# Empty turns ahead of the first matmuls in each batch's transforms, the three uses of one PSUM bank moved within a block, and a down projection four steps behind

## The chip, the cores and the metric

The kernel runs on one core of one Trainium2 chip. The metric is device time in microseconds (us), the median of several executions.

## What is computed

The reference gates a long convolution and puts an MLP behind it, cut to what matters:

```python
h_filt = (np.maximum(pos_emb @ w1, 0.0) @ w2) * np.exp(-0.01 * pos)[:, None]   # 12480 x 128
u = x * v                                                # x, v: 4 batches x 12480 x 128
y = irfft(rfft(u, n=2*S) * rfft(h_filt, n=2*S))[:, :S]   # along the 12480 positions
t = (x * y).reshape(49920, 128)
h = t @ w_in                                             # 128 -> 2048
g = np.where(h > 0, h, np.exp(np.minimum(h, 0)) - 1)     # ELU
return g @ w_out                                         # 2048 -> 128
```

## The kernel before

The convolution is done with discrete Fourier transforms written as matmuls, in two stages with a round trip through DRAM between them. In fp32 a matmul is done as three (`mm3`, lines 53 to 55): operands are split into a rounded part (names ending in `_h`) and a remainder (`_l`), and high by high, low by high and high by low are summed.

For one batch, `stage1` takes 15 groups of 4 positions: `load` brings `xt` and `vt` (SP's queue), `gate` multiplies them on GpSimd (line 102, in place in `vt`), `split` rounds to `u_h` on ScalarE and takes the remainder `u_l` on VectorE, and four `mm3` per group write `aps`, which ScalarE and VectorE copy to `a_sb`; `store` writes it to DRAM, `a_d`. `stage2` takes 52 groups: it loads a table `t`, the stored `al` and the filter's spectrum `f`, rounds the table to `th` and `tl`, multiplies (`xps`), forms products `p` with the spectrum on VectorE and sums them on GpSimd (lines 420 and 421), transforms back (`bps`) and stores to `b_d`. Both are generators: each `yield` ends a piece, and whoever drives them gets one piece at a time.

Batch 0 goes through both stages alone, together with the filter and the splitting of the weights. Then the class `Mlp` runs 960 steps: 120 blocks (30 for each batch) of 4 x 104 tokens, 8 steps a block, each step for 256 of the 2048 hidden features. Step (j, c) issues, in this order:

- `up_proj`: six matmuls of 416 columns to `fps` (two buffers while transforms run, a third after), then two ScalarE instructions for `n` (lines 551 and 552);
- `split_lo` of two steps earlier: VectorE's remainder `g_l` (line 567);
- `elu`: VectorE's `g` (line 558) and GpSimd's cast to `g_h` (line 561);
- `down_proj` of `LAG` steps earlier: six matmuls that add to `ops`; behind the last of a block ScalarE copies `ops` to `o_sb`;
- pieces of the next batch's transforms (`side`), as many as keep their count at `SHARE` times the steps of this batch so far, until they run out. Blocks of batch 0 run beside the transforms of batch 1, and so on; those of batch 3 run alone;
- at fixed steps c of a block the work that prepares and ends blocks: `conv_out` of the next block (the last inverse transform, `yps`, six matmuls, and the gate `att`), `load` for the block three on, `split_b`, `transp` (four transposes to `tps`, then `t_h` and `t_l`), `finish` of the previous block (four transposes to `otp`, copied to `ost`), and `store`, the output transfer.

`yps`, `tps` and `otp` share one PSUM bank, the pool `psm` with one buffer. Every engine works through its instructions in program order, and so does SP's queue of transfers; the order in which this code is written is thus the order on each engine.

Of the kernel before, what the change touches and what calls it, by code (L numbers as in the profile page):

```python
# [27 lines left out]
DFF = 2048  # L28
NF = DFF // 128
NP = NF // 2  # L30
LAG = 3
NBK = 2 * NG
SHARE = 1.04
FWD = ((0, 1), (2, 0))
INV = ((3, 4), (5, 3))

# [2 lines left out]
def fftconv_gate_elu_mlp_kernel(ctx: ExitStack, tc: tile.TileContext, x, v, pos_emb, w1, w2,  # L39
# [41 lines left out]
    def stage1(st, h, ps_pool, ps_tag, first):  # L81
# [6 lines left out]
        def load(g):  # L88
            if g >= NG:
                return  # L90
            xt = xv.tile([N1, 2, G, D], F32, tag="xt", name="xt")
            vt = xv.tile([N1, 2, G, D], F32, tag="vt", name="vt")
            nc.sync.dma_start(out=xt, in_=xq[:, :, h, g * G:(g + 1) * G, :])
            nc.sync.dma_start(out=vt, in_=vq[:, :, h, g * G:(g + 1) * G, :])
            ld[g] = (xt, vt)

        def gate(g):
            if g >= NG:
                return
            xt, vt = ld[g]  # L100
            e = nc.vector if first and g < 2 else nc.gpsimd
            e.tensor_tensor(out=vt, in0=xt, in1=vt, op=ALU.mult)

        def split(g):
            if g >= NG:
                return
            vt = ld.pop(g)[1]
            u_h = up.tile([N1, 2, G, D], F32R, tag="u_h", name="u_h")
            u_l = up.tile([N1, 2, G, D], F32R, tag="u_l", name="u_l")
            copy(u_h, vt)  # L110
            nc.vector.tensor_tensor(out=u_l, in0=vt, in1=u_h, op=ALU.subtract)
            us[g] = (u_h, u_l)
# [7 lines left out]
        if first:  # L120
            filt = Filter(st)
            for g in range(4):
                filt.load(g)
                if g < 3:
                    load(g)
                filt.load_w(g)
            gate(0)
            gate(1)
            for q in range(3):
                filt.step(0, q)  # L130
        else:
            load(0)
            load(1)
            gate(0)
            gate(1)
        split(0)
        for g in range(NG):
            if first:
                gate(g + 2)
            u_h, u_l = us.pop(g)  # L140
            for i in range(4):
                r, w = divmod(i, 2)
                f = FWD[w][r]
                if w == 0:
                    a_sb = ap.tile([N1, G, Z, 2, D], F32 if first else F32R, tag="a_sb", name="a_sb")
                if first:
                    q = 2 * g + r
                    filt.step(q + 1, 2 * w)
                ps = ps_pool.tile([N1, 512], F32, tag=ps_tag, name="aps")
                mm3(ps, dft_h[:, f, :], dft_l[:, f, :], u_h[:, w], u_l[:, w])  # L150
                src = ps.rearrange("p (n d) -> p n d", n=G)
                if first and w == 0:
                    nc.vector.tensor_copy(out=a_sb[:, :, 0, w], in_=src)
                else:
                    copy(a_sb[:, :, 0, w], src)
                if not first:
                    nc.vector.tensor_tensor(out=a_sb[:, :, 1, w], in0=src, in1=a_sb[:, :, 0, w], op=ALU.subtract)
                if first:
                    if w == 0:
                        filt.step(q + 1, 1)  # L160
                        filt.load(q + 4)
                        filt.load_w(q + 4)
                    else:
                        filt.transform(q)
                        filt.weights(q)
                        filt.split_w(q - 1)
                if w == 0:
                    store()
                else:
                    stores.append((g, r, a_sb))  # L170
                if i == 0:
                    load(g + (3 if first else 2))
                if i == 1:
                    split(g + 1)
                if i == 2 and not first:
                    gate(g + 2)
                yield
# [143 lines left out]
    def stage2(st, h, ps_pool, ps_tag, first):  # L321
# [125 lines left out]
            load_t(g)  # L447
        for g in range(d):
            load_a(g)
        split_t(0)  # L450
        split_a(0)
        for g in range(NK):
# [19 lines left out]
    class Mlp:  # L472
        def __init__(self, st):
            self.xp = st.enter_context(tc.tile_pool(name="xp", bufs=3))
            self.bl = st.enter_context(tc.tile_pool(name="bl", bufs=2))
            self.b0 = st.enter_context(tc.tile_pool(name="b0", bufs=2))
            self.tq = st.enter_context(tc.tile_pool(name="tq", bufs=2))
            self.ep = st.enter_context(tc.tile_pool(name="ep", bufs=2))
            self.gp = st.enter_context(tc.tile_pool(name="gp", bufs=4))
            self.op = st.enter_context(tc.tile_pool(name="op", bufs=2))  # L480
            self.psf = st.enter_context(tc.tile_pool(name="psf", bufs=2, space=PS))
            self.pso = st.enter_context(tc.tile_pool(name="pso", bufs=1, space=PS))
            self.psm = st.enter_context(tc.tile_pool(name="psm", bufs=1, space=PS))

        def run(self, side, alone):
# [108 lines left out]
            def store():  # L594
                if outs:
                    j, o = outs.pop(0)
                    b, w, n = blocks[j]
                    nc.sync.dma_start(out=oq[:, w, b, n * G:(n + 1) * G, :], in_=o)
# [10 lines left out]
            done = 0  # L609
            for s in range(len(steps) + LAG):  # L610
                now = steps[s] if s < len(steps) else None
                if s == (NB - 1) * per:
                    psf2 = alone()
                if now:
                    up_proj(*now)
                if 2 <= s <= len(steps) + 1:
                    split_lo(*steps[s - 2])
                if now:
                    elu(*now)
                if s >= LAG:  # L620
                    down_proj(*steps[s - LAG])
                p, q = divmod(s, per)
                if q == 0:
                    done = 0
                while p in side and done < (q + 1) * SHARE:
                    done += 1
                    if next(side[p], None) is END:
                        del side[p]
                if now:
                    j, c = now  # L630
                    if c == 1:
                        conv_out(j + 1)
                        load(j + 3)
                    if c == 2:
                        split_b(j + 2)
                    if c == 4:
                        transp(j + 1)
                    if c == 5:
                        finish(j - 1)
                    if c == 7:  # L640
                        store()
            finish(ALL - 1)
            store()

# [92 lines left out]
```

## Time and profile before

| what | value |
|---|---|
| median of three runs | 3637.33 us (3637.32 to 3637.77) |
| the profiled execution: its time, its span | 3646.31 us, 3644.5 us |
| mean granted TensorE clock | 0.967 |
| TensorE matmul busy | 3434.0 us, 94% |
| TensorE weight load busy | 3158.4 us, 87% |
| VectorE busy | 3136.5 us, 86% |
| ScalarE busy | 2418.3 us, 66% |
| GpSimd busy | 2276.2 us, 62% |
| transfers | 646.29 MB, 177 GB/s as a mean |

In the profile's rows PE is TensorE's matmul, PEld its weight load, DVE VectorE, ACT ScalarE, POOL GpSimd and SPq the queue of transfers that SyncE issues. A row of the timeline has its start, its duration, the engine and line, the instruction with output<-inputs, and in brackets how long the engine stood idle before it and what ended that. Matmuls overlap in a pipeline, so a row's duration is longer than the distance to the next. In the trace the first step of the MLP runs at 553.4 us; the pieces of batch 1's transforms run beside it from there, the first matmuls of those of batches 2 and 3 start at 1402.9 and 2213.5 us. The last store of each batch's second stage is issued at 1312.0, 2124.2 and 2934.1 us; from there to the next start the MLP is alone.

### The profile page before, as it was taken

To read this page: it belongs to the slowest core of one execution; us is meant where nothing else is said; L and a number is where in the kernel's file an instruction comes from. 1 tells how busy PE (TensorE), PEld (TensorE's weight loads), DVE (VectorE), ACT (ScalarE), POOL (GpSimd) and SP (SyncE) were. 2 spreads that over 40 slices of the span, in tenths; PEclk is the share of its full clock that TensorE was granted. 3 is DMA by queue.
4 is the path that set the end of the run, shared out by engine and by line. 5 is a ranking of instruction groups with operands and counts; after the bars stand their busy time and mean duration, and the time that the engine had idled before them with its cause. 6 is when DMAs were issued, how large, how long until landed. Compare 5 with 4: busy or idle time off the path is not lost.

```text
span 3644.5 us, 53113 instructions
## 1 busy us (share of the span) xinstructions
PE 3434.0 (94%) x18444; PEld 3158.4 (87%) x18444; DVE 3136.5 (86%) x3941; ACT 2418.3 (66%) x3290; POOL 2276.2 (62%) x1578
## 2 busy tenths in 40 slices
PE   7887878989999999989999999989999999999999
PEld 5666767879998998879999998879999999999998
DVE  5647988989999988989999988979999988888887
ACT  3334546866666677866666677866666677777776
POOL 3406875857777765557766756657666655655555
PEclk8769998999999999999999999999999999999999
DMA  6648886767777735778888846778888832222220
GB/s 186 185 127 241 267 242 194 222 181 201 203 205 208 201 109 165 242 202 220 238 221 229 227 114 185 241 199 225 233 228 232 237 88 60 59 66 60 69 59 24
DMA packets 383995, 646.29 MB, mean 177 GB/s; under 512 B 24679, under 2 KB 170439, under 8 KB 374367
## 3 DMA queue, kind: packets, MB, share of 16 engines
q1 hardware_dynamic: 383305, 642.73, 62.4%
q8 instruction: 146, 2.39, 0.3%
q14 instruction: 123, 1.00, 0.1%
q10 hardware_dynamic: 421, 0.16, 0.0%
HBM read 412.76 MB, written 230.03 MB: 176 GB/s over the span
## 4 chain that ended last, share of the span: by engine, by line
PE 76%; DVE 8%; ACT 4%; DMA 4%; issue 4%; POOL 3%; SPq 0%; POOLq 0%; DVEq 0%; ACTq 0%
PE fps L53 9%; PE fps L55 9%; PE fps L54 9%; PE ops L53 9%; PE ops L54 9%; PE ops L55 8%; PE bps L439 4%; DVE g_l L567 2%; PE xps L53 2%; PE xps L54 2%; PE xps L55 2%; PE yps L53 2%; PE yps L54 2%; PE yps L55 2%; PE otp L589 1%
## 5 line engine op out<-in xcount | busy, mean ns | idle before, releaser
L561 POOL CAST g_h<-g 128x832 fp32r<-128x832 f32 x960 | 1232.5, 1286 | 1051.3 <-DVE g L558 1050.5
L551 ACT ACTIVATE n<-fps 128x832 f32<-128x832 f32 x960 | 831.9, 867 | 723.1 <-PE fps L55 704.2
L558 DVE SCALAR_TENSOR_TENSOR g<-n,fps 128x832 f32<-128x832 f32 x960 | 975.9, 1017 | 258.5 <-ACT n L552 253.0
L567 DVE TENSOR_TENSOR g_l<-g,g_h 128x832 fp32r<-128x832 f32 x960 | 1097.7, 1143 | 9.3 <-POOL g_h L561 9.3
L552 ACT ACTIVATE n<-n 128x832 f32<-128x832 f32 x960 | 864.4, 900 | 30.5
L53 PE MATMUL fps<-t_h,wi_h 128*128 128x416 f32 x1920 | 716.4, 373 | 0.7 <-ACT t_h L58 0.7
L54 PE MATMUL ops<-g_l,wo_h 128*128 128x416 f32 x1920 | 680.9, 355 | 23.6 <-DVE g_l L567 23.2
L53 PE MATMUL ops<-g_h,wo_h 128*128 128x416 f32 x1920 | 680.4, 354 | 4.7
L55 PE MATMUL fps<-t_h,wi_l 128*128 128x416 f32 x1920 | 677.0, 353 | 0.0
L54 PE MATMUL fps<-t_l,wi_h 128*128 128x416 f32 x1920 | 676.7, 352 | 0.0
L55 PE MATMUL ops<-g_h,wo_l 128*128 128x416 f32 x1920 | 675.1, 352 | 0.0
L420 POOL TENSOR_TENSOR p<-p 120x768 f32<-120x768 f32 x204 | 480.9, 2357 | 69.2 <-DVE p L414 49.3
L54 PEld LDWEIGHTS ops<-g_l,wo_h 128*128 128x128 f32 x1920 | 362.3, 189 | 45.8 <-DVE g_l L567 41.1
L53 PEld LDWEIGHTS fps<-t_h,wi_h 128*128 128x128 f32 x1920 | 364.2, 190 | 21.3 <-ACT t_h L58 1.0
L53 PEld LDWEIGHTS ops<-g_h,wo_h 128*128 128x128 f32 x1920 | 361.6, 188 | 20.0 <-issue 17.5
L54 PEld LDWEIGHTS fps<-t_l,wi_h 128*128 128x128 f32 x1920 | 365.8, 191 | 15.0 <-DVE t_l L540 0.3
L55 PEld LDWEIGHTS fps<-t_h,wi_l 128*128 128x128 f32 x1920 | 362.7, 189 | 2.8
L55 PEld LDWEIGHTS ops<-g_h,wo_l 128*128 128x128 f32 x1920 | 361.5, 188 | 3.4
L412 DVE TENSOR_TENSOR p<-xps,f 120x512 f32<-120x512 f32 x416 | 283.4, 681 | 24.9 <-DMA f<-f_d 14.7
L421 POOL TENSOR_TENSOR p<-p 120x256 f32<-120x256 f32 x204 | 246.0, 1206 | 16.0
L439 PE MATMUL bps<-p,t 120*120 120x256 f32 x832 | 219.1, 385 | 31.5 <-POOL p L421 26.6
L347 DVE TENSOR_TENSOR tl<-t,th 120x360 fp32r<-120x360 f32 x208 | 202.1, 971 | 44.9 <-ACT th L58 31.4
(95 smaller groups left out, 4979.0 us busy)
## 6 DMA issues: line engine op xcount, KB each, us to landing
a_d<-a_sb SPq DMA_DIRECT2D x90, 832.0 KB
al<-a_d SPq DMA_DIRECT2D x156, 480.0 KB
f<-f_d SPq DMA_DIRECT2D x312, 240.0 KB
b_d<-b_sb SPq DMA_DIRECT2D x156, 480.0 KB
b<-b_d SPq DMA_DIRECT2D x90, 832.0 KB
t<-in_tab_dram SPq DMA_DIRECT2D x208, 281.2 KB
xt<-in_x_dram SPq DMA_DIRECT2D x60, 416.0 KB
vt<-in_v_dram SPq DMA_DIRECT2D x60, 416.0 KB
```

The source lines that it names most:

```text
L53: nc.tensor.matmul(out=ps, lhsT=hi, rhs=bh, start=start, stop=False)
L54: nc.tensor.matmul(out=ps, lhsT=hi, rhs=bl, start=False, stop=False)
L55: nc.tensor.matmul(out=ps, lhsT=lo, rhs=bh, start=False, stop=stop)
L412: nc.vector.tensor_tensor(out=p[:, :, :2], in0=ps[:, :, 0:1, :].to_broadcast([RI, TG, 2, D]), in1=f[:, :, r], op=ALU.mult)
L420: e.tensor_tensor(out=q, in0=q, in1=p, op=ALU.add)
L421: e.tensor_tensor(out=q[:, :, 1], in0=q[:, :, 1], in1=q[:, :, 2], op=ALU.add)
L439: nc.tensor.matmul(out=ps[:, o], lhsT=t[:, o, 3 * N2:], rhs=y[:, o, :2], start=True, stop=True)
L551: nc.scalar.activation(out=n, in_=ps[:, :, :NT], func=ACTF.Relu, scale=-1.0)
L552: nc.scalar.activation(out=n, in_=n, func=ACTF.Exp, scale=-1.0)
L558: nc.vector.scalar_tensor_tensor(out=g, in0=n, scalar=-1.0, in1=ps[:, :, :NT], op0=ALU.add, op1=ALU.max)
L561: nc.gpsimd.tensor_copy(out=g_h, in_=g)
L567: nc.vector.tensor_tensor(out=g_l, in0=g, in1=g_h, op=ALU.subtract)
```

## The change

It has four parts. In `stage1`, for batches 1 to 3, seven turns are put in (a `yield` more, so that the next work comes with a later step): four between the loads and the two gates, two between the gates and the split, one between the split and the first group. In `stage2`, six are put between the first loads and the first table split. `SHARE` goes from 1.04 to 1.08. `LAG` goes from 3 to 4, and the pool `gp` of `g_h` and `g_l` from four to five buffers each. And the steps of a block at which the three uses of the `psm` bank stand change from 1, 4 and 5 to 0, 3 and 6, with `load` at 0; the output's `store` goes from step 7 to step 1 of the next block, with one more behind the loop.

```diff
--- before.py
+++ after.py
@@ -28,9 +28,9 @@
 DFF = 2048
 NF = DFF // 128
 NP = NF // 2
-LAG = 3
+LAG = 4
 NBK = 2 * NG
-SHARE = 1.04
+SHARE = 1.08
 FWD = ((0, 1), (2, 0))
 INV = ((3, 4), (5, 3))
 
@@ -131,9 +131,15 @@
         else:
             load(0)
             load(1)
+            for _ in range(4):
+                yield
             gate(0)
             gate(1)
+            yield
+            yield
         split(0)
+        if not first:
+            yield
         for g in range(NG):
             if first:
                 gate(g + 2)
@@ -447,6 +453,9 @@
             load_t(g)
         for g in range(d):
             load_a(g)
+        if not first:
+            for _ in range(6):
+                yield
         split_t(0)
         split_a(0)
         for g in range(NK):
@@ -476,7 +485,7 @@
             self.b0 = st.enter_context(tc.tile_pool(name="b0", bufs=2))
             self.tq = st.enter_context(tc.tile_pool(name="tq", bufs=2))
             self.ep = st.enter_context(tc.tile_pool(name="ep", bufs=2))
-            self.gp = st.enter_context(tc.tile_pool(name="gp", bufs=4))
+            self.gp = st.enter_context(tc.tile_pool(name="gp", bufs=5))
             self.op = st.enter_context(tc.tile_pool(name="op", bufs=2))
             self.psf = st.enter_context(tc.tile_pool(name="psf", bufs=2, space=PS))
             self.pso = st.enter_context(tc.tile_pool(name="pso", bufs=1, space=PS))
@@ -628,17 +637,18 @@
                         del side[p]
                 if now:
                     j, c = now
-                    if c == 1:
+                    if c == 0:
                         conv_out(j + 1)
                         load(j + 3)
+                    if c == 1:
+                        store()
                     if c == 2:
                         split_b(j + 2)
-                    if c == 4:
+                    if c == 3:
                         transp(j + 1)
-                    if c == 5:
+                    if c == 6:
                         finish(j - 1)
-                    if c == 7:
-                        store()
+            store()
             finish(ALL - 1)
             store()
```

The line numbers of the changed file are higher by up to ten. Three places, in the order of one engine's instructions, before and after:

GpSimd where batch 2's transforms start (`g_h<-g` is a cast of one MLP step, `xN` so many in a row; `vt<-xt,vt` is the gate of one group), before:

```order
L561 CAST g_h<-g 128x832 x22
L102 TENSOR_TENSOR vt<-xt,vt 104x1024 x2
L561 CAST g_h<-g 128x832
L102 TENSOR_TENSOR vt<-xt,vt 104x1024
L561 CAST g_h<-g 128x832 x4
```

and after:

```order
L570 CAST g_h<-g 128x832 x25
L102 TENSOR_TENSOR vt<-xt,vt 104x1024 x2
L570 CAST g_h<-g 128x832 x5
L102 TENSOR_TENSOR vt<-xt,vt 104x1024
L570 CAST g_h<-g 128x832 x4
```

The first two gates stand three steps later, and five casts instead of one lie between them and the third gate.

GpSimd where the second stage of the same batch takes over (the last `vt` belongs to the first stage, the first `p` to the second), before:

```order
L102 TENSOR_TENSOR vt<-xt,vt 104x1024
L561 CAST g_h<-g 128x832 x4
L102 TENSOR_TENSOR vt<-xt,vt 104x1024
L561 CAST g_h<-g 128x832 x10
L420 TENSOR_TENSOR p<-p 120x768
L421 TENSOR_TENSOR p<-p 120x2x128
```

and after:

```order
L102 TENSOR_TENSOR vt<-xt,vt 104x1024
L570 CAST g_h<-g 128x832 x3
L102 TENSOR_TENSOR vt<-xt,vt 104x1024
L570 CAST g_h<-g 128x832 x16
L426 TENSOR_TENSOR p<-p 120x768
L427 TENSOR_TENSOR p<-p 120x2x128
```

Between the last gate and the first product stand sixteen steps of the MLP instead of ten.

TensorE at the end of a block's down projection, with no transforms beside it (the first row is the last matmul of the block before into `ops`, the last row the first of the next block), before:

```order
L55 MATMUL ops<-g_h,wo_l 128x416
L53 MATMUL fps<-t_h,wi_h 128x416
L54 MATMUL fps<-t_l,wi_h 128x416
L55 MATMUL fps<-t_h,wi_l 128x416
L53 MATMUL fps<-t_h,wi_h 128x416
L54 MATMUL fps<-t_l,wi_h 128x416
L55 MATMUL fps<-t_h,wi_l 128x416
L53 MATMUL ops<-g_h,wo_h 128x416
```

and after:

```order
L55 MATMUL ops<-g_h,wo_l 128x416
L545 MATMUL tps<-id_sb,att 128x104 x4
L53 MATMUL fps<-t_h,wi_h 128x416
L54 MATMUL fps<-t_l,wi_h 128x416
L55 MATMUL fps<-t_h,wi_l 128x416
L53 MATMUL fps<-t_h,wi_h 128x416
L54 MATMUL fps<-t_l,wi_h 128x416
L55 MATMUL fps<-t_h,wi_l 128x416
L53 MATMUL ops<-g_h,wo_h 128x416
```

The four transposes `tps` of the next block now stand between the two down projections.

## The prediction

> **What bounds the kernel now.** I read the forty slices first, then tables of stretches, then the rows around each hole in them, and last the totals of waits. The slices' PE row, the column header, and nine stretches (length, busy us of each engine with its instructions, granted clock, share of the transfer engines, GB/s):
>
> ```profile
> PE   7887878989999999989999999989999999999999
> core 0: us, PE busy (x) PEld busy (x) DVE busy (x) ACT busy (x) POOL busy (x), PEclk, DMA share, GB/s
> 555.00:575.00 20.00, 10.38 (x33) 7.73 (x32) 8.68 (x8) 7.40 (x10) 6.51 (x5) 0.58 0.61 148
> 760.00:785.00 25.00, 13.55 (x60) 12.21 (x59) 10.10 (x15) 8.32 (x12) 5.36 (x5) 0.73 0.87 218
> 1395.00:1415.00 20.00, 12.24 (x43) 9.94 (x43) 11.58 (x12) 7.47 (x10) 9.86 (x7) 0.74 0.52 142
> 1600.00:1620.00 20.00, 8.77 (x41) 7.67 (x40) 6.75 (x11) 4.84 (x7) 3.02 (x2) 0.74 0.86 230
> 2205.00:2225.00 20.00, 12.24 (x47) 10.04 (x47) 12.03 (x13) 8.14 (x11) 9.86 (x7) 0.74 0.56 147
> 2410.00:2430.00 20.00, 8.72 (x33) 7.50 (x32) 6.29 (x10) 3.92 (x6) 3.02 (x2) 0.66 0.86 218
> 800.00:1300.00 500.00, 480.21 (x2731) 453.33 (x2730) 479.31 (x615) 338.17 (x451) 370.96 (x257) 1.00 0.73 204
> 1640.00:2100.00 460.00, 457.20 (x2625) 438.06 (x2624) 432.26 (x591) 311.01 (x419) 318.85 (x231) 1.00 0.83 228
> 2960.00:3600.00 640.00, 636.56 (x3406) 607.20 (x3405) 529.40 (x557) 478.41 (x589) 379.47 (x248) 1.00 0.26 61
> ```
>
> After the first 15% (batch 0's transforms, untouched) TensorE is nearly always at work, so whatever shortens the kernel must be a stop of TensorE. The slices dip in six places: the first six stretches. Each batch's transforms stop it twice, when their first stage starts (555, 1395, 2205) and when the second takes over (760, 1600, 2410). The clock drops there too, to 0.58 to 0.74 as a mean. Between the holes two regimes show. In 1640:2100 (second stage of batch 2's transforms beside the MLP) TensorE is busy 457 of 460 us: nothing to gain. In 800:1300 (the same for batch 1, where the MLP also splits batch 0's blocks on ScalarE and GpSimd) it lacks 20 us, and VectorE lacks 21: both are near their limit. In 2960:3600 the MLP runs alone: 3406 matmul records in 640 us, 0.188 us each. That is my price of a matmul at full clock.
>
> What a hole costs is its length less its matmuls at 0.188: 20 - 33 x 0.188 = 13.8; 25 - 60 x 0.188 = 13.7; then 11.9, 12.3, 11.2 and 13.8. In all 76.7 us, the slow clock behind each hole included.
>
> Why TensorE stops at a takeover, in the timeline's rows of TensorE and of SP's queue (start, duration):
>
> ```profile
> 1598.76 0.40 PE L55 MATMUL aps<-u_h,dft_l 104*104 104x512 f32 x1
> 1601.09 0.35 PE L55 MATMUL ops<-g_h,wo_l 128*128 128x416 f32 x1
> 1600.84 0.30 SPq L117 DMA_DIRECT2D a_d<-a_sb  x1
> 1607.58 0.34 SPq L361 DMA_DIRECT2D al<-a_d  x1
> 1612.68 0.54 PE L53 MATMUL xps<-al,th 120*120 120x256 f32 x1 [11.23 <-DMA f<-f_d]
> 1615.79 0.63 PE L54 MATMUL yps<-b,dft_h 104*104 104x512 f32 x1
> ```
>
> The last first-stage matmul starts at 1598.76 and ends at about 1599.0. Its result is stored at 1600.84. The load al, which needs that store landed, can be issued only at 1607.58, and the first second-stage matmul runs at 1612.68: 13.7 us after the last of the first stage. In program order a single MLP step stands between, done at 1601.09+. The 512-column matmul behind the hole takes 0.63 where one before it took 0.40.
>
> Why it stops at a start:
>
> ```profile
> 1396.34 0.35 PE L55 MATMUL ops<-g_h,wo_l 128*128 128x416 f32 x1
> 1399.42 4.65 POOL L102 TENSOR_TENSOR vt<-xt,vt 104x1024 f32<-104x1024 f32 x2
> 1401.79 1.06 ACT L58 ACTIVATE u_h<-vt 104x1024 fp32r<-104x1024 f32 x1 [4.40 <-POOL vt L102]
> 1402.90 0.76 PE L53 MATMUL aps<-u_h,dft_h 104*104 104x512 f32 x1 [6.21 <-ACT u_h L58]
> 1405.20 0.75 PE L54 MATMUL aps<-u_l,dft_h 104*104 104x512 f32 x1 [1.55 <-DVE u_l L111]
> ```
>
> The first piece is put into the program right behind its own loads: GpSimd's two products (4.65 us), ScalarE's rounding, VectorE's remainder, with the matmuls behind each, and all other TensorE work queued behind those.
>
> **The change, part by part.** *Empty pieces at a start.* Loads, products, rounding and first matmuls now have MLP steps between them: 7 of them before the first aps. For batches 2 and 3 the loads also leave earlier, since no later output store stands ahead of them on SP. What stays: the two products hold GpSimd 4.65 us in one piece, so the next cast g_h is late by that less the idle time GpSimd has in a step, about 1 us. VectorE's g_l waits behind that cast, and the two fps buffers pass on a part. I keep 1.5 us a start. The gain is 11.9 - 1.5 + 11.2 - 1.5 = 20.1.
>
> Batch 1's start also is the MLP's own, with empty queues:
>
> ```profile
> 555.60 0.55 PE L55 MATMUL fps<-t_h,wi_l 128*128 128x416 f32 x1
> 563.51 0.76 PE L53 MATMUL aps<-u_h,dft_h 104*104 104x512 f32 x1 [7.37 <-ACT u_h L58]
> L551 ACT ACTIVATE n<-fps 128x832 f32<-128x832 f32 x960 | 831.9, 867 | 723.1 <-PE fps L55 704.2
> L552 ACT ACTIVATE n<-n 128x832 f32<-128x832 f32 x960 | 864.4, 900 | 30.5
> L558 DVE SCALAR_TENSOR_TENSOR g<-n,fps 128x832 f32<-128x832 f32 x960 | 975.9, 1017 | 258.5 <-ACT n L552 253.0
> ```
>
> The 7.4 us between these two TensorE rows go. But four steps (three before) now pass without a down projection to fill them: with two fps buffers, two steps take 6 x 0.188 + 0.87 + 0.90 + 1.02 = 3.9 us, so one takes 1.96 and TensorE idles 0.83 of it, 3.3 us for four; and the first twelve matmuls run at 0.55 instead of 0.35, 2.4 us. Of 13.8 us I count 8.1.
>
> *Empty pieces at a takeover.* Six whole MLP steps now stand between the last aps and the first xps: 72 matmuls, six of conv_out and four transposes, 82 x 0.188 = 15.4 us against the 13.7 that the chain of store and loads took. The margin is 1.7 us; VectorE may finish the last a_sb later than before, so I keep 1 us each: 13.7 + 12.3 + 13.8 - 3 = 36.8. On SP the stage's loads stay right behind the last store, ahead of the MLP's, so the chain begins no later. Should the cover fail, al is late next.
>
> *SHARE.* 13 more pieces a batch and 1.08 a step: the transforms end at step 213 instead of 209 of 240, three steps before the first load of the next batch's b, which is needed 16 steps later: nothing. Mixed steps fall from about 208 to 201 a batch and lone ones rise by seven. Where TensorE is the bound this costs nothing; in batch 1's period, where VectorE is, I take 1 us (bounds 0 and 3).
>
> *LAG and the five g_h and g_l buffers.* The down projection takes a remainder that is two steps old, not one. These waits of the whole kernel, and two of 800:1300, price it and the next part:
>
> ```profile
> PE ops L54 <- DVE g_l L567: 23.2, 40, 1.2
> PE otp L589 <- DVE t_l L540: 12.7, 21, 1.7
> PEld ops L53 <- issue: 17.5, 41, 0.4
> ```
>
> ```profile
> PE ops L54 <- DVE g_l L567: 11.8, 16, 1.2
> DVE g L558 <- ACT n L552: 20.7, 34, 1.3
> ```
>
> TensorE waits 23.2 us in all for g_l, 11.8 of it in 800:1300. Outside, a step of slack covers delays of at most 1.2 us: I take 7 of 11.4. Inside, VectorE has only those 20.7 us of idle time, and some waits will move to fps buffers: 5 of 11.8. Sum 12; ends 3 and 23. The buffers themselves add no wait: the cast into the fifth needs a down projection two steps back.
>
> *The one bank (psm) for yps, tps and otp*, written at steps 1, 4, 5 of a block before and 0, 3, 6 now. The transposes otp stood one step behind tps and waited 12.7 us for t_l to release the bank. With three steps between, and two from otp to the next yps, I take 10 (ends 4 and 12.7). A second effect, in a lone step, in the rows of ScalarE and TensorE:
>
> ```profile
> 1382.53 0.50 ACT L58 ACTIVATE o_sb<-ops 128x416 f32<-128x416 f32 x1
> 1382.73 0.34 PE L55 MATMUL fps<-t_h,wi_l 128*128 128x416 f32 x1
> 1383.17 0.43 PE L53 MATMUL ops<-g_h,wo_h 128*128 128x416 f32 x1
> ```
>
> A block's first down projection waits for ScalarE's copy o_sb, which empties its bank: 0.44 us between matmul starts where 0.19 is usual. Before, only the next six matmuls stand between; now the four tps transposes (four records, 0.7 us) stand there too, and cover the 0.25 us. The list above has 41 such waits: 41 x 0.25 = 10 us (ends 4 and 17.5). Output stores six steps earlier or later are covered: nothing else needs them. A last step more to drain also costs nothing, as it fills waits for g_l at the end.
>
> The sum: 20.1 + 8.1 + 36.8 + 12 + 10 + 10 - 1 = 96 us. The profiled execution took 3646.3 us (span 3644.5), 9.0 above the median of the runs, 3637.3; I take the same gain from the median: 3541.
>
> **The rivals.** *Everything goes*: the holes but for the MLP's own start (71), 12.7, 23.2 and 10: 117 us, 3520. For it: TensorE is full in 1640:2100, so it can be. Against: VectorE's 21 idle us in batch 1's period.
>
> *Transfers become late.* The rows for this and the last rival (g_l and the products p by form, in 800:1300, then in 1640:2100; then two long pieces of the chain that ended last):
>
> ```profile
> L567 DVE TENSOR_TENSOR g_l<-g,g_h 128x832 fp32r<-128x832 f32 x141 | 173.6, 1231 | 0.0
> ```
>
> ```profile
> L567 DVE TENSOR_TENSOR g_l<-g,g_h 128x832 fp32r<-128x832 f32 x136 | 152.9, 1125 | 0.0
> L420 POOL TENSOR_TENSOR p<-p 120x768 f32<-120x768 f32 x47 | 119.5, 2542 | 5.5 <-DVE p L414 2.4
> ```
>
> ```profile
> 954.15 3.07 DVE g_l L567
> 1844.94 12.62 DMA al<-a_d
> ```
>
> Stage two already moves 228 GB/s at a share of 0.83, and once an al took 12.6 us instead of the 5.1 above. If it does so at each takeover, the hole is 7.5 - 1.7 = 5.8 us and brings back the slow clock (about 1.8): 20 us more than I kept, 3561. If instead 4% more pieces a step find no bandwidth, some 0.1 us on each of 145 steps in two batches cost 30: 3571. Against: 1600:1620 reaches 0.86 and 230 GB/s even with a hole.
>
> *The holes stay*, because the loads still leave late: only 12 + 10 + 10 remain, 3605. Against: nothing in SP's order delays them.
>
> *Slower.* GpSimd's p takes 2.54 us, and a g_l that meets GpSimd's work takes 3.07 (954.15) where the mean is 1.13 to 1.23. If the shifted steps put one g_l of each round of the second stage behind p, in batches 2 and 3 too, 104 rounds at 2 us more make 208, less VectorE's idle (460 - 432)/136 = 0.2 us on 290 steps: 150 net, 3691. It makes the kernel slower from about 80 of the 104 rounds. Against: the remainder stays two steps behind its elu, so its place beside p does not move. The Trainium skill's page "SBUF — State Buffer" (section "SBUF: two separate sides") says why such a meeting hurts: VectorE with two SBUF inputs and GpSimd share a port pair under an exclusive lock, and the later one blocks for the other's whole instruction. By that rule slack in the down projection can't shorten VectorE's work in batch 1's period, and the 5 us I took there would be 0: 3546. The rows agree as far as g_l is longer, 1231 against 1125 ns, where GpSimd has more to do.
>
> **How the numbers follow.** Forecast 0.64, its own range 3525 to 3559; everything goes 0.13; transfers 0.16; holes stay 0.03; slower 0.03; the last 0.01 for other cancelling losses. About 0.2%, 7 us, is what a measurement of this kernel tells from none. Faster is all but the slower rival and cancelling cases: 0.95; same 0.02, slower 0.03. The range takes in both outer rivals' centres, 3520 and 3571, with a few us for the unknown ends: 3512 to 3578.
>
> **What would show it.** Right: no dip of the slices or the clock behind the MLP's first slice; the first xps of a batch within 2 us of the matmul before it; otp's wait for t_l and the 41 waits on o_sb gone from the list; g_l's halved; 800:1300's counterpart still short of full. Wrong: a wait of xps for al or f of over 3 us at each takeover, al's waits in the second stage rising, or g_l well over 1231 ns in batches 2 and 3.

## The result: 56 us faster, of the 96 forecast

The changed kernel takes 3581.8 us (median of 4 runs, 3574.1 to 3589.3), the kernel before 3637.6 (4 runs, 3637.3 to 3642.0). The ratio is 0.984, with a 95% interval from 0.982 to 0.987. The direction was as forecast. The gain of 56 us is little more than half of the forecast one, and the time lies 4 us above the predicted range.

The profiled execution of after took 3583.0 us, with a span of 3581.2 us. That span is 63.3 us shorter than the one of before, but 4.8 us of it fall ahead of the MLP (its first n, ScalarE's first read of fps, comes at 551.4 instead of 556.2 us), in batch 0's stages, which the change doesn't touch. From there on 58.5 us are gained.

The slices of after, TensorE and its clock:

```profile
PE   7887888999999999999999999999999999999999
PEclk7789998999999999999999999999999999999999
```

The dips at the starts and takeovers no longer show at this grain. Nine stretches of the same kind as those of before (columns as there: length, then busy us and instructions of PE, weight loads, VectorE, ScalarE and GpSimd, clock, transfer share, GB/s):

```profile
551.40:571.40 20.00, 14.12 (x66) 11.36 (x66) 16.19 (x13) 14.33 (x17) 14.86 (x8) 0.98 0.44 105
775.00:800.00 25.00, 21.56 (x112) 20.74 (x111) 19.68 (x25) 15.04 (x21) 15.54 (x10) 0.86 0.69 174
1382.00:1402.00 20.00, 17.37 (x84) 15.52 (x83) 18.24 (x17) 14.37 (x19) 13.94 (x8) 0.91 0.27 75
1592.00:1612.00 20.00, 18.24 (x98) 17.52 (x97) 16.11 (x20) 13.04 (x18) 10.78 (x8) 0.91 0.84 224
2176.00:2196.00 20.00, 17.39 (x84) 15.62 (x84) 18.08 (x16) 14.71 (x20) 14.33 (x8) 0.91 0.28 78
2387.00:2407.00 20.00, 18.24 (x98) 17.45 (x97) 15.71 (x21) 12.95 (x19) 11.33 (x9) 0.91 0.93 223
800.00:1300.00 500.00, 481.47 (x2753) 457.00 (x2752) 490.64 (x619) 339.36 (x454) 374.92 (x258) 1.00 0.74 205
1640.00:2100.00 460.00, 453.60 (x2613) 434.51 (x2612) 433.75 (x591) 307.62 (x415) 314.38 (x228) 1.00 0.82 229
2960.00:3560.00 600.00, 600.00 (x3239) 578.82 (x3238) 503.61 (x531) 454.82 (x560) 362.24 (x236) 1.00 0.24 60
```

Four things are to be seen. Each hole has shrunk (those of batches 2 and 3 to 2 to 3 us without TensorE), but the clock in them is still 0.86 to 0.91 as a mean, but for the MLP's own start. Batch 1's second stage (800:1300) is no fuller than before, 481.5 us against 480.2, while VectorE is up from 479 to 491 of 500. Batch 2's second stage (1640:2100), which was full at 457.2 of 460, has lost 3.6 us. And where the MLP runs alone, TensorE has no idle time left.

TensorE's new waits, from the list of waits, and its matmuls on g_l from the groups (in each list: us in total, times, longest; in the group: busy, mean ns, idle before):

```profile
PE fps L53 <- DVE g L567: 21.2, 29, 1.5
PE xps L53 <- DMA al<-a_d: 10.1, 10, 2.1
PE aps L54 <- DVE u_l L111: 8.4, 4, 2.6
PE xps L53 <- ACT th L58: 7.3, 5, 1.9
PE aps L53 <- DVE a_sb L163: 7.3, 10, 1.6
```

```profile
L54 PE MATMUL ops<-g_l,wo_h 128*128 128x416 f32 x1920 | 674.8, 351 | 0.7 <-DVE g_l L576 0.7
```

The old waits are gone: g_l from 23.2 to 0.7 us, t_l (12.7) and the 41 waits on o_sb off the list. Five others, 54 us in all, stand in their place. Of before's list only these three answer to them, 10 us; waits of fps for g and of aps for a_sb aren't on it:

```profile
PE aps L54 <- DVE u_l L111: 5.9, 4, 2.3
PE xps L53 <- DMA al<-a_d: 3.3, 4, 1.7
PE xps L53 <- ACT th L58: 1.1, 1, 1.1
```

To put a size on each part I took, from the rows of TensorE, the time from each matmul's start to the next less the usual spacing of its kind (0.188 us for the 416-column ones, 0.234 for aps, 0.120 for xps, 0.25 for bps), and added it up by place. A sum comes out a little below zero where spacings are tighter than usual. One period is the 240 MLP steps beside one batch's transforms; the start is steps 0 to 12 and the takeover 52 to 75.

| TensorE time lost, us | before | after | gained | forecast |
|---|---|---|---|---|
| start, batch 1 | 15.4 | 9.4 | 6.0 | 8.1 |
| starts, batches 2 and 3 | 11.9 + 11.2 | 4.2 + 4.4 | 14.5 | 20.1 |
| takeovers, batches 1, 2, 3 | 17.7 + 12.5 + 13.4 | 7.7 + 3.9 + 3.8 | 28.2 | 36.8 |
| rest of batch 1's period | 27.4 | 25.4 | 2.0 | } 21 |
| rest of batch 2's and 3's | 2.7 + 0.3 | 3.0 + 2.8 | -2.8 | } |
| MLP alone | 9.7 | -0.7 | 10.4 | 10 |
| sum | | | 58.3 | 96 |

### The profile page after: what moved, and what is told of

Its sections match the earlier page's. It is cut to its first block, busy times and chain, and to the rows that moved or that the text cites. A ratio compares the mean times of both kernels' runs of the same rounds, so it can differ in the third digit from the quotient of the medians.

```text
span 3581.2 us, 53363 instructions
## 1 busy us (share of the span) xinstructions
PE 3411.3 (95%) x18444; PEld 3153.7 (88%) x18444; DVE 3156.0 (88%) x3941; ACT 2416.0 (67%) x3290; POOL 2280.5 (64%) x1578
## 3 DMA queue, kind: packets, MB, share of 16 engines
q1 hardware_dynamic: 383305, 642.73, 63.3%
## 4 chain that ended last, share of the span: by engine, by line
PE 60%; DVE 9%; DMA 7%; issue 4%; ACT 1%; POOL 1%; SPq 1%; POOLq 0%; DVEq 0%; ACTq 0%
PE fps L53 8%; PE fps L55 8%; PE fps L54 8%; PE ops L53 7%; PE ops L54 7%; PE ops L55 7%; DMA al<-a_d 4%; PE bps L445 3%; DVE g_l L576 3%; DVE g L567 2%; PE xps L53 2%; PE xps L55 2%; PE xps L54 2%; DMA vt<-in_v_dram 2%; PE yps L53 1%
## 5 line engine op out<-in xcount | busy, mean ns | idle before, releaser
L576 DVE TENSOR_TENSOR g_l<-g,g_h 128x832 fp32r<-128x832 f32 x960 | 1111.2, 1157 | 19.6 <-POOL g_h L570 19.6
L561 ACT ACTIVATE n<-n 128x832 f32<-128x832 f32 x960 | 864.5, 901 | 30.5
L53 PE MATMUL fps<-t_h,wi_h 128*128 128x416 f32 x1920 | 715.6, 373 | 22.4 <-DVE g L567 21.2
L54 PEld LDWEIGHTS fps<-t_l,wi_h 128*128 128x128 f32 x1920 | 364.6, 190 | 13.4 <-DVE t_l L549 0.3
L445 PE MATMUL bps<-p,t 120*120 120x256 f32 x832 | 219.5, 386 | 30.5 <-POOL p L427 26.1
L353 DVE TENSOR_TENSOR tl<-t,th 120x360 fp32r<-120x360 f32 x208 | 214.5, 1032 | 25.6 <-ACT th L58 25.4
```

The source lines that it names most:

```text
L53: nc.tensor.matmul(out=ps, lhsT=hi, rhs=bh, start=start, stop=False)
L54: nc.tensor.matmul(out=ps, lhsT=hi, rhs=bl, start=False, stop=False)
L445: nc.tensor.matmul(out=ps[:, o], lhsT=t[:, o, 3 * N2:], rhs=y[:, o, :2], start=True, stop=True)
L561: nc.scalar.activation(out=n, in_=n, func=ACTF.Exp, scale=-1.0)
L576: nc.vector.tensor_tensor(out=g_l, in0=g, in1=g_h, op=ALU.subtract)
```

## The experiments

Each experiment's time is compared with runs of the kernel before on the same chip, and the ratio's 95% interval stands in brackets. A period below is the time from its first n (ScalarE's first read of fps) to the next period's first, read from the timeline. The front of the program scatters: in eleven of the profiles, whatever the kernel, the first MLP step comes between 544.8 and 557.7 us (three others, named below, come earlier). That is one reason why the periods tell more than the totals. Each period comes from one profile; those that an edit leaves alone repeat to 1.5 us (794.4 in after and vx, 795.6 and 795.9 in dv).

| period, us | b1 | b2 | b3 | alone |
|---|---|---|---|---|
| before | 839.4 | 810.6 | 809.8 | 616.6 |
| after | 821.3 | 794.4 | 794.4 | 607.8 |
| h_only | 832.2 | 793.0 | 790.6 | 616.5 |
| l_only | 838.7 | 805.8 | 802.6 | 617.1 |
| p_only | 845.2 | 816.2 | 810.5 | 617.7 |
| lp | 834.8 | 810.5 | 808.6 | 607.2 |
| hl | 827.0 | 790.3 | 788.2 | 617.1 |
| tk | 817.8 | 798.0 | 790.2 | 607.3 |
| st | 823.5 | 789.3 | 794.6 | 607.3 |
| ao | 823.7 | 787.0 | 785.3 | 607.3 |
| vx | 862.4 | 818.7 | 794.4 | 607.3 |
| dv | 803.6 | 795.6 | 795.9 | 607.8 |
| aob | 838.2 | 805.4 | 805.2 | 616.6 |
| best | 813.3 | 779.8 | 782.6 | 607.3 |

### Which part brings what

**h_only**: the empty turns and SHARE alone.

```
 after, with
-LAG = 4            +LAG = 3
-gp: bufs=5         +gp: bufs=4
 and conv_out, load at step 1, split_b 2, transp 4, finish 5, store 7, as before
```

> The empty turns and SHARE 1.08 alone, on the kernel before (3637 us). Theory A (the other parts only move waits): the filled holes are nearly the whole gain of the change, about 48 us, so 3590, and the waits of the down projection for g_l and of otp for t_l stay about as long as before. Theory B (the holes give less than forecast because transfers and the slow clock take it back, and the other parts bring their forecast 32): only some 30 us, 3607.

It took 3594.7 us, 0.989 [0.986, 0.992]: 39 us gained, between the two accounts (48 and 30). The waits for g_l and t_l stay, as the first said (30.5 and 9.8 us). The turns are the bulk of the change.

**l_only**: the down projection four steps behind, with five buffers, alone. **p_only**: the spread uses of the bank alone. **lp**: both.

```
 before, with
 l_only, lp:  LAG 3 -> 4, gp bufs 4 -> 5
 p_only, lp:  conv_out, load at step 0, store 1, transp 3, finish 6
```

> LAG 4 and five buffers alone. Theory A: 0 to 4 us faster (3633 to 3637): the 23 us of waits for g_l vanish from the list and about as much appears as the up projection waiting for VectorE's g; the weight load's 41 waits of 0.4 us behind o_sb stay. Theory B: 12 us faster, 3625.

> The bank's uses at steps 0, 3 and 6 alone, with LAG 3. Theory A: 2 to 6 us faster (3631 to 3635): otp's wait for t_l goes, but in batch 1's period VectorE sets the pace; the 41 waits behind o_sb stay, since with LAG 3 the copy falls into step 2 and tps into step 3, behind the next down projection. Theory B: 10 us faster, 3627.

> LAG 4 with five buffers and the bank's uses at steps 0, 3 and 6, without empty turns, SHARE 1.04. Theory A: about 12 us, 3625, nearly all of it from the copy o_sb being covered by the four tps transposes in lone steps; waits for g_l are replaced by waits of the up projection for g. Theory B: 32 us, 3605.

l_only took 3635.0 us, 1.000 [0.999, 1.002]; p_only 3656.4, 1.005 [1.003, 1.006]; lp 3620.4, 0.996 [0.994, 0.998]. TensorE's waits by kernel, from the lists (l_only, p_only, lp in this order):

```profile
PE otp L589 <- DVE t_l L540: 28.6, 31, 2.3
```

```profile
PE ops L54 <- DVE g_l L567: 42.8, 60, 1.4
PE xps L53 <- DMA f<-f_d: 25.2, 2, 14.8
PE xps L53 <- DMA al<-a_d: 17.8, 5, 14.1
```

```profile
PE fps L53 <- DVE g L558: 23.2, 31, 1.5
```

Slack in the down projection alone takes the wait for g_l away, and the wait for t_l rises from 12.7 to 28.6 us. Spreading the bank alone takes the wait for t_l away, and the one for g_l rises from 23.2 to 42.8. With both, the wait stands at fps, for g to release its buffer: 23.2 us, where before shows none. Each time VectorE's work is what is waited for; only the tile changes. p_only was expected a little faster and came out slower, by 17 us by the ratio and 22 by the medians. Its list shows the cause in part: 20 us more on g_l, and takeovers that last longer (al up to 14.1, f up to 14.8 us). That its earlier load of the MLP's tiles stands just ahead of the takeover's transfers on SP is seen in its order, but that this is what lengthens them was only argued.

**hl**: after, without the spread of the bank.

```
 after, with conv_out, load at step 1, split_b 2, transp 4, finish 5, store 7, as before
```

> The changed kernel with the bank's uses put back to steps 1, 4 and 5 (and load and store with them). Theory A: lone steps lose the 10 us of the covered o_sb; beside batch 1's transforms the waits of the up projection for g turn back into otp waiting for t_l, at about the same sum; al waits less: 5 to 12 us slower than the changed kernel, 3587 to 3594. Rival (the spread itself saves what otp waited, as forecast): 20 us slower, 3602.

It took 3584.3 us, 0.987 [0.983, 0.990], hardly different from after. Two of its waits:

```profile
PE otp L598 <- DVE t_l L549: 21.4, 25, 1.6
PE fps L53 <- DVE g L567: 8.4, 10, 2.1
```

The wait for t_l is back, and the one for g is down from 21.2 to 8.4 us: about the same sum. Two stretches where the MLP runs alone, of hl and of lp:

```profile
2960.00:3560.00 600.00, 596.49 (x3191) 568.80 (x3191) 498.60 (x523) 452.11 (x552) 355.36 (x233) 1.00 0.24 59
```

```profile
2960.00:3560.00 600.00, 600.00 (x3244) 578.73 (x3243) 504.06 (x532) 454.57 (x560) 361.41 (x237) 1.00 0.25 63
```

Without the spread the lone period is at 617.1 us (hl, l_only), without LAG 4 at 617.7 (p_only), and with both at 607.2 (lp). So the wait on o_sb goes only by both together, and brings its 10 us. But hl's periods of batches 2 and 3 are 4 and 6 us shorter than those of after, and its waits for al are down from 10.1 to 4.5 us: the spread gives back there what it gains in the lone steps. In batch 1's period the two parts together do bring something: after is 5.7 us shorter than hl there, and lp 4.6 us shorter than before.

### What is left of the holes

The takeover of batch 2 in after, TensorE's rows and one of SP's queue:

```profile
1597.01 0.35 PE L55 MATMUL ops<-g_h,wo_l 128*128 128x416 f32 x1
1598.91 0.38 PE L53 MATMUL xps<-al,th 120*120 120x256 f32 x1 [1.54 <-ACT th L58]
1601.83 0.55 PE L55 MATMUL fps<-t_h,wi_l 128*128 128x416 f32 x1
1603.45 0.35 PE L54 MATMUL ops<-g_l,wo_h 128*128 128x416 f32 x1
```

```profile
1590.47 0.34 SPq L367 DMA_DIRECT2D al<-a_d  x1
```

The load al leaves 8.4 us before its use: the chain of store and load, which made this hole, is covered as forecast. What stops TensorE now is ScalarE's rounding of the first table, th, issued in the same turn as the matmul that needs it. The stop is 1.5 us, but from 1600 until 1603.2 the rows last 0.55 us instead of 0.35, with starts 0.35 apart instead of 0.19.

**tk**: the first table is rounded one turn ahead of the first group.

```
         if not first:
-            for _ in range(6):
+            for _ in range(5):
                 yield
         split_t(0)
+        if not first:
+            yield
         split_a(0)
```

> The changed kernel with the first table of a batch's second stage rounded one turn earlier (five turns, the rounding, one turn, the first matmuls). Theory A: what is left of each takeover is the rounding of the table in the turn of the first matmuls (a stop of 1.5 us) and the slow clock that follows it (some 1.7 us): about 3 times 3.3, 10 us less than the changed kernel's 3582, so 3572, and no xps waits for th. Rival: al lands just then, so xps waits for al instead, and no more than 3 us are gained.

It took 3577.8 us (3553.1 to 3588.7), 0.984 [0.980, 0.988]: by the runs alone, no more than after. Its takeover:

```profile
1585.00:1607.00 22.00, 22.00 (x129) 21.30 (x128) 20.59 (x27) 17.03 (x23) 12.82 (x11) 1.00 0.82 205
```

TensorE is busy all through, at full clock. From the n of step 52 to that of step 75 the takeovers last 73.1, 70.6 and 70.6 us against 77.8, 74.3 and 74.3: 12.1 us gained, nearly the whole of what was left at batches 2 and 3. Of this, batch 2's second stage gave 6 us back (433.4 us against 427.5 for steps 75 to 200). Its waits for al are no longer than in after (4.8 against 5.2 us), but a wait of 2.3 us for b_sb is new, and two stretches at half clock of 3.4 us each fall into it, where after has none.

The start of batch 2 in after (GpSimd, TensorE, VectorE, in order of time):

```profile
1384.70 6.28 POOL L102 TENSOR_TENSOR vt<-xt,vt 104x1024 f32<-104x1024 f32 x2
```

```profile
1389.02 0.47 PE L53 MATMUL aps<-u_h,dft_h 104*104 104x512 f32 x1
1392.12 0.76 PE L54 MATMUL aps<-u_l,dft_h 104*104 104x512 f32 x1 [2.63 <-DVE u_l L111]
1394.30 0.55 PE L54 MATMUL fps<-t_l,wi_h 128*128 128x416 f32 x1
```

```profile
1389.61 2.46 DVE L111 TENSOR_TENSOR u_l<-vt,u_h 104x1024 fp32r<-104x1024 f32 x1
```

The two products, 4.65 us before, now hold GpSimd 6.28 us. The first matmuls stand one turn behind the split, but VectorE comes to the remainder u_l, which the second of them needs, only 0.6 us after the first has begun.

**st**: the two products two turns apart.

```
-            for _ in range(4):
+            for _ in range(3):
                 yield
             gate(0)
-            gate(1)
             yield
             yield
+            gate(1)
+            yield
         split(0)
```

> The changed kernel with the two first gates of a batch two turns apart (three turns, first gate, two turns, second gate, one turn, rounding) instead of back to back. Theory A: the stop left at a start is VectorE's remainder u_l, late because GpSimd holds 6.3 us in one piece and VectorE's g_l waits for it: 2.6 us of stop and about 1.2 of slow clock go at batches 2 and 3, 7 us less, 3575. Rival: the stop is u_l's own duration in the turn of the rounding, and stays: 3582.

It took 3585.5 us, 0.987 [0.986, 0.989]: no gain. Its start, GpSimd's and VectorE's rows:

```profile
1391.18 2.37 POOL L102 TENSOR_TENSOR vt<-xt,vt 104x1024 f32<-104x1024 f32 x1
```

```profile
1391.32 3.30 DVE L111 TENSOR_TENSOR u_l<-vt,u_h 104x1024 fp32r<-104x1024 f32 x1
```

The second product now meets u_l itself, which takes 3.30 us instead of 2.46. The waits for u_l came to 9.5 us instead of 8.4 (4.4 at batch 1's start and 2.3 at the others, where after has 2.6 at each), so my account, in which the pair of products is what has to be broken up, did not hold. best, below, keeps the pair and puts one more turn behind the split: there the wait is gone.

### The transfers of the second stage

SP's queue in after, one of the late loads al, and the piece of the chain that ended last that it makes:

```profile
1920.24 0.34 SPq L342 DMA_DIRECT2D t<-in_tab_dram  x1
...
1921.09 0.44 SPq L367 DMA_DIRECT2D al<-a_d  x1
...
1927.05 0.33 SPq L342 DMA_DIRECT2D t<-in_tab_dram  x1
1927.47 0.39 SPq L435 DMA_DIRECT2D b_d<-b_sb  x1
1928.05 0.49 SPq L367 DMA_DIRECT2D al<-a_d  x1
```

```profile
1928.05 11.46 DMA al<-a_d
```

In program order the table's load t for three groups on stands ahead of al, and it needs a buffer that only the inverse transform of the group before sets free. al, whose own buffer may long be free, leaves right behind t.

**ao**: the table's load behind al's. **aob**: the same swap alone, on the kernel before.

```
         for g in range(NK):
-            load_t(g + 3)
             split_t(g + 1)
             ...
             load_a(g + d)
+            load_t(g + 3)
             spectrum(g)
```

> The changed kernel with the table's load put behind the load of al in each group of the second stage. Theory A: in SP's queue the table's load waits for its buffer, which the inverse transform of the previous group frees only at the end of the group, and al stands queued behind it; so al leaves one group (10 us) ahead of its use, about as long as it takes to land. Put ahead, it leaves two groups ahead: the 10 us of xps waiting for al go, 8 to 10 us less, 3573, and the runs scatter less. Rival: the transfers are limited by bandwidth, al lands as late as before: 3582.

> The kernel before with only the table's load put behind that of al. Theory A (the loads of al became late by the change, since groups of the second stage follow one another faster): the kernel before lost only 3 us to al, so at most 5 us faster, 3630 or more. Rival (the queue's order cost as much before, hidden under other waits): 12 us or more faster, 3623 or less.

ao took 3562.0 us (3553.5 to 3575.9), 0.982 [0.979, 0.984]; its interval still touches that of after. Its profile is plain: one wait for al is left (1.9 us, in batch 1's period), and the periods of batches 2 and 3 shorter by 7.4 and 9.1 us. So these loads were late by their place in the queue, not for want of bandwidth. aob took 3629.3, 0.998 [0.996, 1.000], with 5 us less in each of the two periods in its profile, its fastest run of ten. The late load was there before, but it cost little: the waits for al came to 3.3 us. Even these 5 us are not sure, as the profile of before is itself a slow run of its kernel (3646.3 us against a median of 3637.6). The three profiles with this swap are those in which the MLP starts earlier (533.6 us in aob, 542.0 in ao and best). Batch 0's second stage has the same loop, so it may gain too; that wasn't tried apart.

### Who sets the pace beside batch 1's transforms

**vx**: more VectorE work, in batches 0 and 1 alone: the product att is made four times for their blocks, the same values again.

```
-                nc.vector.tensor_tensor(out=a, in0=ps, in1=xt, op=ALU.mult)
+                for _ in range(4 if blocks[j][0] < 2 else 1):
+                    nc.vector.tensor_tensor(out=a, in0=ps, in1=xt, op=ALU.mult)
```

> The changed kernel with VectorE's gate att done four times instead of once in every block of batches 0 and 1 (three times 0.6 us more, 54 us in each of two periods); batch 2's blocks are not changed and serve as a control. Theory A: beside batch 1's transforms VectorE sets the pace, so that period grows by about 45 us (the 54 less what falls on lone steps); beside batch 2's transforms, where TensorE does, the first 25 us are covered, and it grows by 15 to 25; batch 3's period by nothing. In all 60 to 70 us more than the changed kernel, 3645. Rival (TensorE's waits there are a matter of the order of steps, with VectorE's time to spare in both): both periods grow alike and little, under 15 us each, under 3612.

It took 3653.4 us, 1.006 [1.003, 1.009]. One att lasts 0.69 us, so VectorE got 62 us more in batch 1's period and 60 in batch 2's, not the 54 that I had reckoned with. Batch 1's period grew by 41.1 us, batch 2's by 24.3 and batch 3's, where nothing was added, by nothing. vx's list:

```profile
PE fps L53 <- DVE g L568: 51.2, 65, 2.0
```

So VectorE does set the pace in batch 1's period: two thirds of the added work show in the time, and the wait at fps grows from 21.2 to 51.2 us. In batch 2's period three fifths of it hide.

**dv**: the remainder of batch 0's blocks, 28 subtractions of the MLP's input that GpSimd does, done by VectorE as for the first two.

```
-                    e = nc.gpsimd if j > 1 else nc.vector
+                    e = nc.vector
```

> The changed kernel with the remainder of batch 0's blocks (28 more of them, on GpSimd 2.4 us each) taken by VectorE at about 1.2 us. Beside batch 1's transforms VectorE sets the pace, so 34 us of work are added to it; against that GpSimd no longer holds it up there: g_l would fall from about 1231 to 1125 ns and tl from 912 to 583, some 41 us. Theory A: these nearly cancel in that period, -10 to +5 us, and nothing changes elsewhere. Rival (VectorE's waiting behind GpSimd is hidden): the 34 us come on top, 30 us slower than the changed kernel, 3612.

It took 3563.5 us (3548.7 to 3577.8), 0.981 [0.977, 0.985]; this interval touches that of after. Batch 1's period fell by 17.7 us, more than either account allowed, though VectorE got 28 subtractions more, 39.5 us in all. The groups of g_l and tl in 700:1300, first of after, then of dv:

```profile
L576 DVE TENSOR_TENSOR g_l<-g,g_h 128x832 fp32r<-128x832 f32 x170 | 211.9, 1247 | 0.0
L353 DVE TENSOR_TENSOR tl<-t,th 120x360 fp32r<-120x360 f32 x52 | 55.1, 1061 | 0.0
```

```profile
L576 DVE TENSOR_TENSOR g_l<-g,g_h 128x832 fp32r<-128x832 f32 x176 | 197.5, 1122 | 0.0
L353 DVE TENSOR_TENSOR tl<-t,th 120x360 fp32r<-120x360 f32 x52 | 37.3, 720 | 0.0
```

g_l takes 1122 ns as a mean instead of 1247, as in batch 2's period before (1125). tl takes 720 instead of 1061. Over the whole period g_l is 27.4 us less and tl 17.8, together more than the 39.5 us added; with the rest VectorE is busy 773.2 us where it was 785.2. The Trainium skill's page "SBUF — State Buffer" (section "SBUF: two separate sides") has the rule that fits: a VectorE instruction with two SBUF inputs and GpSimd work that reads SBUF hold a shared port in turn, each for its whole instruction. The shorter g_l and tl agree with it; the page gives no price for such a move, and here it pays.

### A version that beats both

**best**: ao, tk and one more empty turn between the first split and the first group of a first stage.

```
         split(0)
         if not first:
             yield
+            yield
 and the edits of ao and tk
```

> The changed kernel with three mends: the table's load behind that of al, the first table rounded one turn earlier, and one more turn between the rounding of the first group and its first matmul (the two first gates back to back, as in the changed kernel). Theory A: what the change still loses at takeovers, at starts and on al adds up to about 16 + 12 + 7 us in the profile; so some 25 to 30 us less than the changed kernel's 3582, 3552 to 3557, ratio to the kernel before 0.977 to 0.980. Rival: each mend only hands the wait on, as with the gates: 3562, no better than the load order alone.

It took 3544.1 us (5 runs, 3538.8 to 3544.9), 0.975 [0.973, 0.978], some 10 us better than expected. One stretch and TensorE's largest wait:

```profile
1600.00:2100.00 500.00, 499.03 (x2873) 479.88 (x2872) 477.52 (x641) 341.78 (x458) 341.11 (x249) 1.00 0.81 222
```

```profile
PE fps L53 <- DVE g L570: 27.1, 26, 2.6
```

Batch 2's second stage is full again, th and al are off the list of waits, u_l is down from 8.4 to 0.5 us, and the wait on VectorE's g, most of it in batch 1's period, is the largest that is left. By themselves ao and tk aren't clear of after's interval; the three edits together are, and bring 38 us by the medians, 33 by the ratios. Of the 44 us between the two profiles 9 fall ahead of the MLP's first n, which the expectation didn't count; why they do wasn't tried.

## Why the prediction was right or wrong

The profile lacks 38 us of the 96: 22 in the waits of the mixed steps and 16 in the holes. Two steps of the prediction failed, and these are the sizes.

*What bounds the kernel, and the holes.* The reading held: the turns alone bring 39 us of the gain (h_only), and the largest term was the takeovers. The chain from store to load is covered by the six steps, the al at the takeover leaves 8.4 us early, and the MLP's own start lost its 7.4 us wait.

*The size of what stays of each hole.* Here the first step failed. I kept 1.5 us a start and 1 us a takeover, 5.7 at batch 1's start. Measured are 4.2 and 4.4 a start, 3.8 to 7.7 a takeover, 9.4 at batch 1's: 33 us against 12 assumed. (The table's places are a little wider than my six stretches: before has 82 us in them, where I priced 76.7.) The holes gave 48.7 us of 65. At a start I had named g_h as what would be late, at a takeover a_sb; it was u_l, one turn ahead of the matmul that needs it, and th, issued in that matmul's own turn. The waits for a_sb came elsewhere, in later groups of the first stage. And I had counted no slow clock behind these rests, only 2.4 us for the MLP's first matmuls. In after seven stretches of 3.41 us at half clock follow the rests of the six places; each costs 1.7 us, 12 us in all. tk shows it: with the table one turn earlier the takeovers got 12.1 us shorter, where the waits of xps for th had been 4.9; four of the seven slow stretches (6.8 us) went with them.

*g_l and otp.* This second step is the larger: 12 and 10 us were counted (21 with SHARE's 1 us off), and the rest of the mixed steps gained -1. The waits did go, as forecast, but they were passed on: g_l to t_l (l_only), t_l to g_l (p_only), both to g (lp, after). The forecast named VectorE's 21 idle us as a limit and then still counted 5 and 10 us beside it. vx shows that VectorE sets the pace there. What the two parts do gain in batch 1's period, some 5 us (lp, hl), goes again in batches 2 and 3, where after waits longer for al than hl does. The sentence with 3546, by which the rule of the Trainium skill on the shared port leaves nothing of the 5 us, went the right way: LAG alone shortens that period by 0.7 us (l_only). It didn't reach the 10 of otp, which failed for the same reason.

*Transfers late.* This rival, 0.16, came true in part, by another mechanism than it said; the sign that I had named, al's waits rising in the second stage, showed (3.3 to 10.1 us). The takeovers' al is not late and the bandwidth suffices; the second stage's al is late by its place behind a load that waits for a buffer (ao), and takes back 7 and 9 us in batches 2 and 3, which ao recovers. So the spread of the bank is worth only some 2.5 us in all by the medians (hl), less than the intervals can tell.

*o_sb.* 10 us counted, 10.4 measured, all in lone steps, by the mechanism named (the four transposes that cover the copy).

*SHARE, the buffers, the output stores*: no wait of theirs is on the list. *Slower*: g_l is at 1243 ns in 800:1300 against 1231, so meeting GpSimd costs there what it did before; nothing of that rival came.

## What to carry to other kernels

A wait that is taken from an engine which follows a slower one comes back at the next tile they share, so ask who sets the pace of the stage before adding up waits, and test it by giving that engine more work. Put every producer of a stage's first matmul far enough ahead of it (here one step for the table, two for u_l), and not only the longest chain: a rest of some 1.8 us can cost as much again in slow clock (the next section says when). In a queue that keeps order, a load that waits for a buffer belongs behind those that don't.

## What the runs showed that I had not expected

- *The clock after a short stop.* The stop of 1.54 us up to 1598.9, with 0.21 us behind it, was followed by a stretch at half clock, and by a clock of 0.91 over 1592:1612; in tk, without the stop, it is 1.00. But a longer stop, 2.09 us up to 2736.9, left the clock at 1.00. Two pairs of neighbouring stretches of 3.41 us in after, around these two stops (columns as above; the clock stands ahead of the last two):

```profile
1596.49:1599.90 3.41, 1.65 (x9) 1.10 (x8) 3.11 (x5) 2.73 (x5) 2.20 (x2) 1.00 0.99 247
1599.90:1603.31 3.41, 3.41 (x15) 3.32 (x14) 3.19 (x5) 0.52 (x1) 0.40 (x1) 0.50 1.03 210
2733.12:2736.53 3.41, 1.70 (x10) 1.35 (x8) 3.03 (x5) 2.28 (x4) 3.33 (x3) 1.00 0.98 247
2736.53:2739.95 3.42, 3.04 (x18) 3.05 (x19) 2.44 (x5) 0.90 (x2) 1.16 (x2) 1.00 0.98 321
```

  The slow stretches of a trace last 3.41 us or a multiple of it and start whole multiples of it apart (608 us, or 178, from 784.1 to 1391.7; 208 us, or 61, from there to 1599.9). So what counts is TensorE's idle time between two marks of this grid, and the second stop is cut by a mark at 2736.5. In the 14 traces, from 560 us on, every such stretch at full clock with more than 1.86 us of idle time in the profile's rows (63 of them) was followed by half clock, and none with less than 1.57; between the two, where both of these lie (1.76 and 1.71 us), 19 were and 15 were not. The Trainium skill's page "TensorE: Matmul & The Clock Gate" (section "Part 1: The HAM clock gate (the "warmup" mystery)") puts the drop behind an idle window of about 3.4 us. Here about half of that was enough, and the measurement decides.
- *A product on GpSimd stretches what VectorE does beside it, and is stretched itself:* the two products took 6.28 us instead of 4.65, u_l 3.30 instead of 2.46.
- *Moving work onto the engine that sets the pace made the period 17.7 us shorter* (dv), as it no longer met that engine from GpSimd.
